# Shared query rows from a second DMA queue, folds on one engine, warming matmuls, and queries held behind keys in an attention and Fourier-mixing kernel

## The chip, the cores and the metric

The kernel runs on one core of a Trainium2 chip. A core has five engines with a queue of instructions each, worked off in order: TensorE (PE in the profile: matmuls, with the weight loads shown apart as PEld), VectorE (DVE), ScalarE (ACT), GpSimd (POOL) and SyncE (SP), which here only issues DMAs. The metric is the device time of one execution in microseconds; the median of the runs shown counts. A profiled execution has its own time, and its span runs from the first to the last instruction.

## The reference

All data are float32. Batch and heads are 8, the sequence 576, the head dimension 64.

```
q_s = exp(q - max over head dim);   q_s /= sum over head dim + 1e-9
k_s = exp(k - max over sequence);   k_s /= sum over sequence + 1e-9
x   = q_s @ (k_s.T @ v)             per head, then heads side by side: (8, 576, 512)
u   = x + real(fft over sequence (fft over the 512 columns (x)))
un  = (u - mean) / sqrt(variance + 1e-6)       per row
out = u + relu(un @ w_ch1) @ w_ch2             w_ch1: 512 x 2048, w_ch2: 2048 x 512
```

## The kernel before

**Tiling.** A batch has 576 rows. 512 of them form four tiles of 128 rows that are mirror images of one another for the Fourier transform; `xpart(b, c, u)` is tile (c, u) of batch b. The remaining 64 rows of each batch are "shared": those of all batches are gathered into one further group of rows, two batches (128 rows) at a time. Queries of a pair of batches for these rows are loaded by `t_rows` with the pieces that `shared` lists: one piece of four rows (0, 32, 64, 96 of the tile, at a stride in memory) and eight of 15 or 16 rows.

**Attention of one batch** (`attention`) is a software pipeline over items: four key items ("k", two heads each), four own query tiles ("q"), and for even batches one shared query tile ("t"). Stages of a key item: load, `k_exp` (maximum on VectorE, exponential with its sum on ScalarE), `k_turn` (five transposes on PE, a copy of four of them to `ks` by ScalarE, L451, and of the fifth by VectorE, L455), `k_times_v` (five matmuls, L463, then two scalings into `kvr`, L466). Stages of a query item: load, `q_exp` (maximum on VectorE L496, subtraction on GpSimd L497, exponential on ScalarE L498, sum, reciprocal and scaling on VectorE L500 to L503), `q_turn` (four transposes L509, a copy L516), `q_times_kv` (L541, a copy of x L543). The shared tile has `t_turn` and `t_fold` (into T and F), and `t_times_kv` closes the batch (L551, L557 and the value `g`, L559 to L562).

**Fourier mixing** (`transform`, `second`, `mix_own`, `mix_shared`). A transform over the sequence and one over the columns are made of folds (sums and differences of mirrored halves) and small matmuls with cosine and sine tables. `transform` first folds the four tiles into `eo[0]` to `eo[3]`: `tokens_folded` (L579), `columns_folded` (L584), `by_frequency` (L590), `columns_again` (L602, L603). The sums of the first two run on GpSimd, the differences on VectorE; `eo[2]` and `eo[3]` feed the sine blocks, `eo[0]` and `eo[1]` the cosine blocks. Then come five blocks of matmuls (L622, L625) in the order 2, 3, 0, 1, 4, each evicted by three ScalarE copies (L628 to L633). `second` multiplies by the column tables (L645, L648), and `added` adds the result to x (L663, L664).

**The feed-forward part.** Seven groups of 512 rows take it in Strassen form, with seven products instead of eight (`up` L814, `down` L850), reading prepared weights from memory. The first batch takes it plainly (`plain`): 16 up steps (L744, relu L746) and 64 down steps (L753). While it runs, the weights, which lie in memory as 64-bit words, are converted to float32 (`convert`: ScalarE L313 and L321, VectorE L314, L316, L318, GpSimd L322, 32 pieces), combined for Strassen (`combine`, L328 to L338) and written back to memory. Between the down steps lie the attention, mixing and norm of the second batch, placed by the list `gaps` (how many down steps before each further side step).

**Order.** The program writes steps in a fixed order; the framework then lists each engine's instructions by data dependences and expected costs, and inserts semaphore waits. `wait_for(t, raws)` adds an artificial dependence: VectorE operations that read a word of `t` and write back unchanged words of the named tiles, so that whatever uses these comes after `t`. Before the change it holds the first four weight pieces behind the folds (L596). `hold` keeps buffers of the second batch's keys and queries unused until the up steps 12 and 14. `first` issues all loads of the first batch on SP: keys 0 and 1, all values, keys 2 and 3, own queries, shared queries, tables, weights.

The second batch's third and fourth key, and its last query tile, use the space of the normalised input of the up stage (`spare`), which is free after its last matmul.

## Time and profile before

| | |
|---|---|
| median of 3 runs | 1154.71 us (1154.26 to 1156.3) |
| the profiled execution | 1154.03 us |
| its span | 1152.2 us |
| TensorE busy | 1099.4 us (95%) |
| VectorE busy | 556.5 us (48%) |
| ScalarE busy | 352.5 us (31%) |
| GpSimd busy | 378.3 us (33%) |
| first up matmul (L744) | at 63.41 us |
| first down matmul (L753) | at 121.35 us |
| first Strassen matmul (L814) | at 210.32 us |

The page gives busy times by engine, and the span in 40 slices with a digit for the busy share of each. "PEclk" is the TensorE clock that was granted, in tenths of full speed. In the timeline each row has a start and a length in us, then the engine, the line of the program, the operation, output and inputs by the program's names with their shapes, a count, and in brackets the idle time of the engine before it with what ended that. A row may merge several instructions. A float32 matmul appears as two records, so that a down step of one matmul with 512 columns is two records, 0.857 us together at full clock.

### The profile page before, as it was taken

What the parts mean: (1) busy time and instruction counts of PE and PEld (TensorE: products, weight loads), DVE (VectorE), ACT (ScalarE), POOL (GpSimd) and SP (SyncE); (2) the same over time, 40 slices, a digit from 0 to 9 for tenths busy, and PEclk for the clock granted to TensorE, in tenths of its full rate; (3) what the DMA queues carried; (4) which work ended last, traced back from release to release, by engine and by line L of the source; (5) the groups of instructions that cost most, each with busy time, mean ns of one, the idle gap of its engine ahead of it and who ended that gap; (6) DMA issues with size and microseconds to landing.
All of it is one profiled execution on the core that took longest, in us unless ns stands there. A gap on an engine that the chain in (4) does not pass through costs nothing.

```text
span 1152.2 us, 14397 instructions
## 1 busy us (share of the span) xinstructions
PE 1099.4 (95%) x5432; PEld 918.5 (80%) x5432; DVE 556.5 (48%) x1136; ACT 352.5 (31%) x699; POOL 378.3 (33%) x344
## 2 busy tenths in 40 slices
PE   6499799998999999999999999999999999999997
PEld 5444465787888988888889888888889888888886
DVE  6888748368343634376334733583434353202301
ACT  4575322344123512242225222341233142201200
POOL 3446624237103520255023601361033303402320
PEclk9789899999999999999999999999999999999999
DMA  8556777255345534553365434543454344444451
GB/s 293 168 168 212 247 275 229 80 187 187 140 142 201 202 113 145 185 188 146 120 206 196 154 116 153 200 178 137 142 181 151 115 140 171 165 155 153 148 183 55
DMA packets 92101, 193.75 MB, mean 168 GB/s; under 512 B 23296, under 2 KB 58624, under 8 KB 84864
## 3 DMA queue, kind: packets, MB, share of 16 engines
q1 hardware_dynamic: 90424, 192.05, 49.0%
q8 instruction: 43, 0.70, 0.2%
q10 hardware_dynamic: 1608, 0.79, 0.2%
q14 instruction: 26, 0.21, 0.1%
HBM read 168.69 MB, written 28.31 MB: 171 GB/s over the span
## 4 chain that ended last, share of the span: by engine, by line
PE 76%; DVE 8%; ACT 2%; POOL 1%; issue 1%; DMA 1%; DVEq 0%; POOLq 0%; SPq 0%
PE bb L814 13%; PE bb L850 13%; PE bc L850 10%; PE bc L814 8%; PE ba L814 8%; PE ba L850 7%; PE acc L463 2%; PE bc L753 2%; PE acc L541 2%; PE acc L622 2%; PE acc L625 1%; PE acc L645 1%; PE tr L714 1%; PE tr L450 1%; PE tr L509 1%; PE bb L753 1%
## 5 line engine op out<-in xcount | busy, mean ns | idle before, releaser
L814 PE MATMUL bb<-unT,big 128*128 128x256 f32 x768 | 187.8, 381 | 0.0
L850 PE MATMUL bb<-big 128*128 128x256 f32 x768 | 172.8, 379 | 0.0
L814 PEld LDWEIGHTS bb<-unT,big 128*128 128x128 f32 x768 | 142.8, 190 | 23.4 <-DVE u L782 4.0
L850 PEld LDWEIGHTS bb<-big 128*128 128x128 f32 x768 | 145.1, 190 | 20.0
L814 PE MATMUL bc<-unT,big 128*128 128x256 f32 x512 | 125.4, 379 | 0.0
L814 PE MATMUL ba<-unT,big 128*128 128x256 f32 x512 | 124.0, 379 | 0.0
L328 POOL TENSOR_TENSOR big<-big 128x512 f32<-128x512 f32 (+1 forms) x38 | 46.1, 1214 | 234.0 <-ACT big L826 233.6
L850 PE MATMUL bc<-big 128*128 128x256 f32 x512 | 116.5, 379 | 0.5 <-DVE x L867 0.5
L826 ACT ACTIVATE big<-big 128x512 f32<-128x512 f32 x96 | 60.5, 630 | 183.9 <-DVE big L825 183.4
L850 PE MATMUL ba<-big 128*128 128x256 f32 x512 | 114.1, 379 | 0.0
L850 PEld LDWEIGHTS bc<-big 128*128 128x128 f32 x512 | 95.9, 190 | 14.2 <-DVE x L867 0.9
L850 PEld LDWEIGHTS ba<-big 128*128 128x128 f32 x512 | 95.9, 190 | 12.3
L814 PEld LDWEIGHTS bc<-unT,big 128*128 128x128 f32 x512 | 95.4, 190 | 12.4
L814 PEld LDWEIGHTS ba<-unT,big 128*128 128x128 f32 x512 | 95.2, 190 | 11.8
L786 DVE TENSOR_TENSOR u<-bb,s 128x512 f32<-128x512 f32 x40 | 27.6, 690 | 141.1 <-PE bb L850 80.0
L336 POOL TENSOR_TENSOR unT<-unT 128x512 f32<-128x512 f32 x8 | 14.2, 1776 | 171.8 <-DVE unT L335 171.8
L862 POOL TENSOR_TENSOR x<-x,u 128x512 f32<-128x512 f32 x14 | 17.8, 1269 | 149.9 <-DVE u L786 118.8
L782 DVE TENSOR_TENSOR u<-bb,s 128x512 f32<-128x512 f32 x40 | 27.6, 691 | 79.7 <-PE bb L814 42.4
L825 DVE TENSOR_TENSOR big<-bc,u 128x512 f32<-128x512 f32 x64 | 44.1, 689 | 22.9 <-PE bc L814 22.0
L778 ACT COPY s<-ba 128x512 f32<-128x512 f32 x40 | 23.4, 586 | 90.3 <-PE ba L850 47.1
L497 POOL TENSOR_TENSOR q<-q,qm 128x512 f32<-128x512 f32 x30 | 31.5, 1058 | 58.7 <-DVE qm L496 30.3
L329 POOL TENSOR_TENSOR big<-big 128x512 f32<-128x512 f32 (+1 forms) x38 | 48.0, 1264 | 2.3 <-DVE big L330 0.4
(222 smaller groups left out, 1673.2 us busy)
## 6 DMA issues: line engine op xcount, KB each, us to landing
big<-w1s SPq DMA_DIRECT2D x64, 896.0 KB, 4.7
big<-w2s SPq DMA_DIRECT2D x56, 1024.0 KB, 4.9
big<-in_w_dram SPq DMA_DIRECT2D x21, 512.0 KB, 4.8
k<-in_kT_dram SPq DMA_DIRECT2D x26, 288.0 KB, 4.1
q<-in_q_dram SPq DMA_DIRECT2D x27, 256.0 KB, 2.8
v<-in_v_dram SPq DMA_DIRECT2D x26, 256.0 KB, 3.8
words<-in_w_dram SPq DMA_DIRECT2D x11, 512.0 KB, 10.4
w2s<-big SPq DMA_DIRECT2D x8, 512.0 KB, 10.4
```

What stands on the lines that cost most here:

```text
L328: e1.tensor_tensor(out=to(4), in0=at(2), in1=at(3), op=ALU.add)
L329: e1.tensor_tensor(out=to(2), in0=at(0), in1=at(2), op=ALU.subtract)
L463: nc.tensor.matmul(pk, lhsT=ks[:, c, :], rhs=v[:, c, :], start=(c == 0), stop=(c == NC - 1))
L497: nc.gpsimd.tensor_tensor(out=heads, in0=heads, in1=spread(m), op=ALU.subtract)
L753: nc.tensor.matmul(po[:], lhsT=h[:, f, i * P:(i + 1) * P], rhs=self.w2sb[:, f, :], start=(f == 0), stop=(f == NF - 1))
L778: nc.scalar.copy(temp("s1"), box["ba"][:])
L782: V.tensor_tensor(out=temp("u2"), in0=box["bb"][:], in1=box["s1"][:], op=ALU.add)
L786: V.tensor_tensor(out=temp("u3"), in0=box["bb"][:], in1=box["s1"][:], op=ALU.add)
L814: nc.tensor.matmul(bank()[:, i, :], lhsT=w[:, WA_AT[m], k * P:(k + 1) * P], rhs=unT[:, B_AT[m], k, :], start=first and i == 0 and k == 0, ...
L825: V.tensor_tensor(out=hp(i), in0=bank[:], in1=u[:], op=ALU.add)
L826: nc.scalar.activation(hp(i), hp(i), ACT.Relu)
L850: nc.tensor.matmul(bank()[:, i, :], lhsT=h[p][:, A_AT[m], i * P:(i + 1) * P], rhs=w[:, p, :], start=first and i == 0 and p == 0, stop=p == ...
```

## The change

All parts concern the first two batches, except that shared queries are loaded in fewer pieces everywhere.

- `t_rows`: four runs of 32 rows on an engine given by the caller, then the one piece of four rows on SP, which overwrites the first row of each run and so waits for it. In `first` the runs are issued by ScalarE ahead of everything, followed by a dummy exponential; the last piece goes out after the first half of the values. The values come in two halves by columns.
- The shared query item stands after the first two keys in the first batch, no longer at the end, and `t_times_kv` comes earlier (step 8).
- `transform` for the first batch: all folds on VectorE, first those of the sine parts (2, 3), then the cosine parts; the hold on the first four weight pieces moves behind the last fold. After each column fold two warming matmuls are issued (`warm`: the tile times the identity, into a PSUM buffer that nobody reads), and after each sum in `mix_own` three. They are ordinary matmuls of 256 columns.
- The second batch: when its third key is turned, `wait_for` makes its four query tiles depend on that key's copy. The copy of the fifth transpose of its keys is made by ScalarE.
- `gaps` begins 2, 2, 2, 2, 2, 8, 2, ... in place of 8, 2, 2, ...

As listed by engine in the built programs: TensorE's queue gets 20 warming matmuls; the second batch's first key transposes stand after 5 down matmuls (11 before); ScalarE's queue has the copies of keys 0 and 1 and the third key's exponential ahead of all query exponentials of that batch (before: three query exponentials ahead of the first copy); of the first four weight conversions VectorE's queue has one complete and the first step of another before the additions to x (before: all four).

```diff
+    def warm(self, t, n):
+        junk = self.turned()
+        for _ in range(n):
+            self.nc.tensor.matmul(junk[:, 0:2, :], lhsT=self.ident[:], rhs=t, start=True, stop=True)
...
+        last = self.t_rows(b, tail, nc.scalar)
+        t = self.small.tile([P, 1], F32, tag="root", name="root", bufs=1)
+        nc.scalar.activation(t[:], self.eps[:], ACT.Exp)
         for r in range(NR):
             load(ks[r], self.kT[b, r * P:(r + 1) * P, :])
-            if r == 1:
-                load(v[:, 0:4, :], self.v[b, 0:512, :].rearrange("(c p) n -> p c n", p=P))
-                load(v[:, 4, :], self.v[b, S - P:, :])
+            if r % 2 == 0:
+                cols = slice(r * P, (r + 2) * P)
+                load(v[:, 0:4, cols], self.v[b, 0:512, cols].rearrange("(c p) n -> p c n", p=P))
+                load(v[:, 4, cols], self.v[b, S - P:, cols])
+                if r == 0:
+                    last()
...
-    def t_rows(self, b, q):
-        for rows, mem in self.shared(self.q, b):
-            self.nc.sync.dma_start(q[rows], mem)
+    def t_rows(self, b, q, e):
+        flat = self.q.rearrange("b s n -> (b s) n")[b * S:(b + 2) * S]
+        for i in range(4):
+            at = i * S // 2 + P
+            e.dma_start(q[i * Q:(i + 1) * Q], flat[at:at + Q])
+        return lambda: self.nc.sync.dma_start(q[0:P:Q], flat[::S // 2])
...
-        items += tail + own if b else own + tail
+        items = items + tail + own if b else items[:2] + tail + items[2:] + own
...
-        return pipelined(items, stages) + [lambda: self.t_times_kv(b)]
+        steps = pipelined(items, stages)
+        steps.insert(len(steps) if b else 8, lambda: self.t_times_kv(b))
+        return steps
...
         nc.scalar.copy(ks[:, 0:4, :], pt[:])
+        if it[1:] == (1, 2):
+            self.wait_for(ks[:, 0, :], [q.bitcast(I32) for q in self.held_back])
...
-        nc.vector.tensor_copy(ks[64:, 4, :], pt[64:, 0, :])
+        copy = nc.scalar.copy if it[1] == 1 else nc.vector.tensor_copy
+        copy(ks[64:, 4, :], pt[64:, 0, :])
...
-            for i, (e, op) in enumerate(((G, ALU.add), (G, ALU.add), (V, ALU.subtract), (V, ALU.subtract))):
+            for i in some:
+                e, op = ((V if b == 0 else G), ALU.add) if i < 2 else (V, ALU.subtract)
                 t = eo[i]
                 e.tensor_tensor(out=t[:, 1:HD], in0=t[:, 1:HD], in1=t[:, D - 1:HD:-1], op=op)
+                if b == 0:
+                    self.warm(t[:, 0:HD], 2)
...
+        def at_first():
+            for some in ((2, 3), (0, 1)):
+                for f in (tokens_folded, columns_folded, by_frequency, columns_again):
+                    f(some)
+            t = self.small.tile([P, 1], F32, tag="root", name="root", bufs=1)
+            V.tensor_scalar(out=t[:], in0=eo[1][:, NN:NN + 1], scalar1=0.0, scalar2=None, op0=ALU.mult)
+            nc.scalar.activation(t[:], t[:], ACT.Sqrt)
+            self.wait_for(eo[1][:, NN:], [self.raws[i] for i in range(4)])
...
         def add(lo, hi):
-            self.added(self.xpart(b, c, 0), lo, hi)
-            self.added(self.xpart(b, c, 1), hi, lo)
+            for u, (f, g) in enumerate(((lo, hi), (hi, lo))):
+                x = self.xpart(b, c, u)
+                self.added(x, f, g)
+                if b == 0:
+                    self.warm(x[:, 0:HD], 3)
...
-            gaps = [8] + [2] * (len(one) - 1) + [3] * 5 + [1] * 4 + [2] * (len(two) - 9) + [1] * 7
+            gaps = [2] + [2] * 4 + [8] + [2] * (len(one) - 6) + [3] * 5 + [1] * 4 + [2] * (len(two) - 9) + [1] * 7
```

The same choice of engine and of `some` stands in `tokens_folded`, `by_frequency` and `columns_again`. The line numbers of the changed program are about 40 higher: L744 becomes L784, L753 L793, L463 L488, L656 L693, L814 L854, L509 L536.

## The prediction

> **What bounds the kernel now.** I read the page's 40 slices first, then the busy time by stretch, the list of waits, and the timeline around the two places where TensorE (PE) is idle. PE is busy 1099.4 of 1152.2 us, so at most 52.8 us of idling can be won, plus what runs at half clock. The slices put nearly all of it at the start and in the fourth and fifth slice:
>
> ```profile
> PE   6499799998999999999999999999999999999997
> DVE  6888748368343634376334733583434353202301
> PEclk9789899999999999999999999999999999999999
> ```
>
> By stretches of 4 us (columns: length, busy us and instructions of PE, weight loads, VectorE, ScalarE, GpSimd, then clock, DMA share, GB/s):
>
> ```profile
> core 0: us, PE busy (x) PEld busy (x) DVE busy (x) ACT busy (x) POOL busy (x), PEclk, DMA share, GB/s
> ...
> 12.00:16.00 4.00, 3.25 (x16) 2.88 (x16) 3.13 (x8) 2.61 (x5) 2.88 (x3) 1.00 0.37 81
> ...
> 36.00:40.00 4.00, 0.00 (x0) 0.00 (x0) 4.00 (x12) 0.00 (x1) 2.47 (x3) 0.59 0.27 69
> ...
> 52.00:56.00 4.00, 0.00 (x0) 0.00 (x0) 4.00 (x13) 1.63 (x3) 0.00 (x0) 0.72 0.57 209
> 56.00:60.00 4.00, 1.42 (x7) 1.42 (x8) 3.96 (x15) 0.86 (x3) 0.00 (x0) 0.50 0.00 0
> 60.00:64.00 4.00, 3.20 (x12) 2.08 (x11) 2.91 (x12) 3.82 (x8) 0.72 (x1) 0.50 0.00 0
> ```
>
> VectorE (DVE) is full while PE has nothing, and the clock is at half when the first dense matmuls (L744) begin at 63.41. The timeline of PE shows the price of that clock, eight matmuls in 5.67 us where the next eight take 3.60:
>
> ```profile
> 63.41 5.67 PE L744 MATMUL ba<-unT,big 128*128 128x512 f32 x8 [0.77 <-ACT unT L718]
> 68.92 3.60 PE L744 MATMUL bb<-unT,big 128*128 128x512 f32 x8
> ```
>
> The second place is the second batch's keys. First the timeline of PE, then that of ScalarE (ACT), in one stretch:
>
> ```profile
> 132.27 1.02 PE L753 MATMUL bc<-big 128*128 128x512 f32 x2
> 137.21 2.08 PE L463 MATMUL acc<-v,ks 128*128 128x128 f32 x8 [3.91 <-ACT ks L451]
> 140.44 0.80 PE L463 MATMUL acc<-v,ks 128*128 128x128 f32 x2 [1.16 <-DVE ks L455]
> ```
>
> ```profile
> 132.75 0.63 ACT L498 ACTIVATE q<-q 128x512 f32<-128x512 f32 x1 [1.99 <-POOL q L497]
> ...
> 136.05 0.63 ACT L498 ACTIVATE q<-q 128x512 f32<-128x512 f32 x1 [1.91 <-POOL q L497]
> 136.58 0.57 ACT L451 COPY ks<-tr 128x512 f32<-128x512 f32 x1
> ```
>
> The copy of the turned keys (L451) stands in ScalarE's queue behind query exponentials that wait for GpSimd; PE waits 3.91 us for it, and 1.16 more for the second copy on VectorE. To price this: the down stage runs from 121.35 to the first L814 at 210.32, 88.97 us. Its PE work at the undisturbed rates of the same timeline is 128 matmul records x 0.429 = 54.9 (3.43 us per eight), keys 4 x (0.55 + 1.11) = 6.6, queries 4 x (0.44 + 0.89) = 5.3, the shared part 1.8, five transform blocks 4.9, three mixes 3.4, turns 1.8: 78.7. So 10.3 us are lost, all between 131 and 151: 5.7 idle (3.91 + 1.16 + 0.67) and 4.6 of half clock.
>
> **What the Trainium skill says.** "TensorE: Matmul & The Clock Gate", section "What's actually happening": the array runs at half clock by default and at full clock after about 3.4 us of sustained activity; the trace agrees (0.50 between 56 and 64, full speed some 5 us into L744). "GPSIMD Engine Reference", section "1. Specifications": GpSimd shares its SBUF interface with VectorE instructions of two SBUF inputs; here L579 takes VectorE 1.21 us beside GpSimd against 0.69 for L503, of the same shape, alone. "DMA: Bandwidth & Descriptors", "Issuing engines are not separate DMA queues": a second issuing engine saves issue time only.
>
> **The front, part by part.** (a) Shared queries: nine pieces held the SP queue 9.07 us (5.07 to 14.14) and DMA sank to 81 GB/s between 12 and 16. Four runs now leave from ScalarE, one from SP. Own queries were fetched before that gap, so they gain nothing from it; tables and weights come up to 9 us earlier, but nobody waits for them. 0.26 MB more stand ahead of keys and own queries: with 336 to 388 GB/s, about +0.7 us. The exponential's table load (1.28, formerly after the first keys) moves ahead of them: about -0.5, hidden later. Taken together nothing, 0 to +1.
> (b) Until the last query is scaled VectorE has its old key and query work and now also the shared part: after the shared rows land (about 9.2, from the bytes ahead of them) two key maxima 1.5, copies 1.2, kv scaling 2.3, query maxima 3.4, sums 3.3, scaling 3.4, small ones 1.8, T and F 1.7, L586 to L589 1.0: 19.6 us. Before, it idled about 3 us in the same stretch; I allow 1, so 29.8 at worst, 29 taken. Then turn 0.63, copy 0.59, product 1.1 and five ScalarE copies of 0.52, partly behind each other: last x at about 34, against 32.0 before.
> (c) Folds on VectorE alone, without a neighbour: 4 x 0.65 + 4 x 0.36 + 4 x 0.37 + 8 x 0.24 = 7.4 us; those of tokens 0 start before the last x, 6 remain: done at 40 to 40.5, before at 41.5. GpSimd's six fold operations go, at no gain beyond this. Eight warming matmuls lie between (0.43 us each at full, 0.86 at half clock); they read what the next fold overwrites, so the last fold may wait 0.5.
> (d) Sines first: blocks 2 and 3 compute from about 38, but ScalarE holds the sqrt table load (1.28) and a value that needs the last fold; from 40.5 it still owes 1.9 (load and value) + five block evictions of 0.75 + three conversion passes of 0.63 = 7.5. First L693 at about 48.4, before (as L656) at 50.86: -2.5. The warm clock hides behind ScalarE here.
> (e) Adds 4.27 and norm 5.04 as before; two conversion steps (1.3) now lie between: VectorE done at 59.0 (before 60.17). Turns at full clock and two copies less ahead: 1.9 for 3.24. L784 (the old L744) starts at about 60.9: -2.5.
> (f) Twelve warming matmuls in the adds: if the clock is full at L784, 5.67 - 3.60 = 2.1 more. Sum of the front: -4.6; bounds +1 (VectorE idles as before, clock cold) and -8.
> (g) The first four conversions move: of their 12 VectorE steps about half come after the norm, some 4 us in a stage (63.4 to 121.35) where VectorE was busy 48.83 of 57.95. Hidden, if the idle 9 us can be filled.
>
> **The second batch.** Key steps come earlier (after 5 instead of 11 down steps), and the queries are held: a VectorE operation that reads the third key's copy writes into all four query tiles, so no query exponential can stand ahead of a key copy; the second copy goes to ScalarE, 0.3 behind the first. Now, from the end of the up stage t: PE reaches the first product (L488) at 5 x 0.857 + 0.55 + 2 x 0.857 = t + 6.5. ScalarE's queue puts the third key's exponential ahead of that copy, and this key's load waits for the up stage to free its buffer and for three query loads: issued at t + 1.5 to 3.3 (before: at t + 3.8), 4.1 to land, maximum 0.74, exponential 0.78, copies 0.9: t + 8 to 10. PE waits 1.5 to 3.5, say 3. Then nothing is late: third copy at t + 15.3, queries released, first one ready 5.5 later (maximum 0.7, GpSimd 1.3, exponential 0.63, sum to scaling 2.2) at t + 21, wanted at t + 26. VectorE is idle some 2 us behind the hold; the last conversion and the kv scaling stand behind it, wanted by nobody before t + 26. With 0.5 of other waits and a third of the half-clock loss (1.4), 4.9 of the 10.3 stay: -5.4. Bounds: -9 (no wait) and 0 (a cold clock and a late key). Further on, folds of this batch start when x is there and take 10.6 as before; PE has 16 us of other work in that place, so nothing becomes late. Later batches: four or five issues less on SP per shared load, where PE is 95 to 100% busy: nothing.
>
> **Sum.** 1154.0 (the profiled execution; span 1152.2) - 4.6 - 5.4 = 1144.0. The median shown is 0.7 above the profiled one: 1144.7. A measurement of this kernel can tell about 0.2%, 2.3 us.
>
> **Rivals.** (1) The stall only moves: the third key's load is what the copies wait for, the clock falls, and the second batch gains nothing; the front alone remains, 1154.7 - 4.6 = 1150. For it: copies still stand behind an exponential that needs a late load. Against: 4.1 us to land from an earlier issue. (2) The front is bound by VectorE all the way and is no shorter (bound +1); the second batch gives 5.4: about 1149. For it: VectorE is at 3.5 to 4.0 of 4 us in most stretches up to 60, and only GpSimd's folds are moved on to it. (3) Slower, by one mechanism: VectorE's conversions fall behind in the up stage, because its idle time there is made of waits in an in-order queue and can't be filled; each us that it is behind at t goes on the third key's maximum, its exponential, all key copies and PE. Beyond t + 6 each us is lost; with the half clock (4.6) and a front gain of 4.6 to eat, it decides from a lag of some 10 us on, and 13 us would give 1158. Against: only 4 us are moved there.
>
> **Chances and range.** Both gains, 1138 to 1149: 0.64. Rival 1: 0.14. Rival 2: 0.10. Rival 3: 0.12. Faster 0.80, same 0.08 (edges of rivals 1 and 2), slower 0.12. The range, 1138 to 1153, reaches from a front of -8 with a mid gain of -8.5 to the weak end of rivals 1 and 2. The likeliest case alone: 1138 to 1149.
>
> **What would show it.** Right: L784 starting near 61 with eight records in 3.6 us; VectorE without GpSimd beside it in the folds, 0.65 each; first L693 near 48; PE's wait before L488 below 4 us and no query exponential ahead of a key copy; clock 1.00 through the down stage; down stage about 84 us. Wrong: a start later than 63, a clock of 0.5 at L784, waits of more than 6 us at L488 or any at L536, VectorE conversions still running 10 us after the up stage, or new PE waits at the transform blocks or the first L854.

## The result, and the profile after

The changed kernel takes 1156.57 us (median, 1154.65 to 1157.65), the kernel before 1155.51 us in the same comparison (1154.26 to 1156.31): a ratio of 1.0008, 95% interval 0.9991 to 1.0026. Nothing was won that can be measured; the prediction was 1144.7 us. The profiled execution took 1157.65 us, its span is 1155.9 us.

The slices of the changed kernel, PE, VectorE and granted clock, answer to the first lines of the prediction:

```profile
PE   5789889999999999999999999999999999999997
DVE  6788856469243634466334832483434343202201
PEclk9999989999999999999999999999999999999999
```

A slice is 28.9 us here. The second rises from 4 to 7, the fifth, where the keys stalled, from 7 to 8 (the prediction named the fourth and the fifth; the fourth stood at 9 in both kernels). But the first falls from 6 to 5, and the third and the sixth from 9 to 8: idle time has moved there. The clock is up in nearly all. By stretches of 4 us in the front (same columns as in the prediction):

```profile
12.00:16.00 4.00, 3.54 (x16) 3.14 (x16) 3.13 (x10) 1.98 (x4) 0.66 (x1) 1.00 1.03 385
36.00:40.00 4.00, 2.67 (x9) 1.66 (x8) 3.16 (x8) 0.59 (x1) 0.00 (x0) 0.86 0.01 3
52.00:56.00 4.00, 4.00 (x21) 3.51 (x20) 4.00 (x13) 0.84 (x3) 0.00 (x0) 1.00 0.26 107
56.00:60.00 4.00, 2.23 (x15) 1.45 (x13) 4.00 (x13) 1.59 (x4) 0.95 (x1) 1.00 0.00 0
60.00:64.00 4.00, 0.78 (x6) 0.42 (x4) 4.00 (x13) 3.05 (x6) 0.52 (x1) 1.00 0.42 131
64.00:68.00 4.00, 3.57 (x5) 1.60 (x6) 4.00 (x8) 4.00 (x8) 2.55 (x2) 0.57 0.30 74
```

DMA moves 385 GB/s where it sank to 81, and PE is busy with warming matmuls and transposes up to 61.6 us. Then it idles until 64.4, and the clock is 0.57 just when the dense matmuls begin. PE's timeline and its list of waits from 50 to 230 us (columns: who waited for whom, us in total, times, longest) say why, and what else is new:

```profile
64.43 5.36 PE L784 MATMUL ba<-unT,big 128*128 128x512 f32 x8 [2.85 <-DVE big L335]
69.62 2.74 PE L784 MATMUL bb<-unT,big 128*128 128x512 f32 x6
```

```profile
PE bc L793 <- POOL big L339: 3.2, 1, 3.2
PE ba L784 <- DVE big L335: 2.9, 1, 2.9
PE acc L568 <- ACT qT L543: 2.8, 1, 2.8
...
PE acc L488 <- ACT ks L472: 1.2, 1, 1.2
```

The wait for the key copy has shrunk from 3.91 + 1.16 to 1.2 us. Three others stand beside it: those before the first up product (L784) and the first down product (L793) were 0.77 us each in the kernel before, and that before the first query product of the second batch (L568) is new. None of the three was in the prediction.

*The first up product.* Its transposed inputs are complete at 62.6, it starts at 64.43. What it waits for, L335, is the last VectorE step of the third weight piece. Up step 0 writes PSUM bank `ba`, and `convert` puts the third piece into the same bank (`ba` is one of the buffers in PSUM, the memory that matmuls write). In the kernel before this conversion was over long before the up stage (VectorE ran it from 44.7 to 47.8 us); now it comes after the norm.

*The first down product.* In the kernel before it waited, too, but little:

```profile
121.35 1.96 PE L753 MATMUL bc<-big 128*128 128x512 f32 x4 [0.77 <-issue]
```

ScalarE's timeline says for what, first before, then after:

```profile
120.10 0.63 ACT L313 ACTIVATE acc<-words 128x512 f32<-128x512 f32 x1 [1.83 <-DMA words<-in_w_dram]
120.67 0.58 ACT L746 ACTIVATE big<-bc 128x512 f32<-128x512 f32 x1
121.26 1.28 ACT L440 ACT_TABLE_LOAD   x1
```

```profile
120.52 0.63 ACT L330 ACTIVATE acc<-big 128x512 f32<-128x512 f32 x1 [3.38 <-DMA big<-in_w_dram]
121.09 0.65 ACT L338 ACTIVATE big<-big 128x512 int32<-128x512 uint32 x1
121.75 1.28 ACT L461 ACT_TABLE_LOAD   x1
123.05 0.78 ACT L461 ACTIVATE k<-k,km 128x576 f32<-128x576 f32 x1
...
123.82 0.57 ACT L786 ACTIVATE big<-bc 128x512 f32<-128x512 f32 x1
```

The first down product writes bank `bc`, which the relu of the 15th up step frees. In both kernels this relu stands in ScalarE's queue behind the conversion of a weight that DMA has not brought yet: before the change the relu is done at 121.25, and the first down product starts at 121.35. In the changed kernel the framework lists the table load for the keys' exponentials and the first of these ahead of the relu as well: it runs at 123.82 for 0.57 us, and the first down product starts at 124.50. The list of waits names GpSimd (L339), whose step ended at 123.96; ScalarE's relu ends later, at 124.39, and with another bank for this product the wait is gone (below). "Perfetto Trace Analysis", section "Tensor Engine Instruction (MATMUL, LD_WEIGHTS)", of the Trainium skill says that ScalarE, VectorE and GpSimd work off their queues strictly in order. The trace agrees: ScalarE idles 3.38 us for a DMA while this relu, which doesn't need it, stands behind.

*The first query product.* ScalarE's timeline shows what stands ahead of the first query copy (L543), and PE's what that costs:

```profile
148.62 0.63 ACT L525 ACTIVATE q<-q 128x512 f32<-128x512 f32 x1 [0.97 <-POOL q L524]
151.00 0.63 ACT L525 ACTIVATE q<-q 128x512 f32<-128x512 f32 x1 [1.74 <-POOL q L524]
155.88 0.63 ACT L525 ACTIVATE spare<-spare 128x512 f32<-128x512 f32 x1 [4.25 <-POOL spare L524]
156.53 0.59 ACT L543 COPY qT<-tr 128x512 f32<-128x512 f32 x1
```

```profile
157.17 2.26 PE L568 MATMUL acc<-kvr,qT 128*128 128x128 f32 x8 [2.76 <-ACT qT L543]
159.22 1.06 PE L536 MATMUL tr<-ident,q 128*128 128x128 f32 x4
160.07 3.54 PE L793 MATMUL ba<-big 128*128 128x512 f32 x4
```

The hold keeps query exponentials from standing ahead of the copies of the first three keys. It lets the last query's exponential (on `spare`) stand ahead of the first query's copy: the same stall one stage further on, with the same half clock behind it (eight L568 records in 2.26 us, at full clock 1.05; four L793 in 3.54, at full clock 1.88).

Summed by stage starts, the first profile of each kernel and, below, a second one (columns in us; "to the end" is from the first Strassen matmul to the end of the span):

| | first up | first down | first Strassen | to the end | span |
|---|---|---|---|---|---|
| before | 63.41 | 121.35 | 210.32 | 941.9 | 1152.2 |
| before, again | 64.36 | 121.64 | 210.56 | 941.3 | 1151.9 |
| changed | 64.43 | 124.50 | 213.98 | 941.9 | 1155.9 |
| changed, again | 63.63 | 122.85 | 210.71 | 942.7 | 1153.4 |

Executions of one kernel differ by some us (those of the kernel before lay between 1151.5 and 1159.6 us over all comparisons), so a difference of 1 or 2 us between two single profiles says little; the verdicts below rest on the ratios, the profiles show the places.

### The profile page after: what moved, and what is told of

Same layout as the page of the kernel before. It is cut to its first block, busy times and chain, and to the rows that moved or that the text cites. A ratio compares the mean times of both kernels' runs of the same rounds, so it can differ in the third digit from the quotient of the medians.

```text
span 1155.9 us, 14469 instructions
## 1 busy us (share of the span) xinstructions
PE 1106.0 (96%) x5472; PEld 922.9 (80%) x5472; DVE 558.2 (48%) x1142; ACT 353.4 (31%) x704; POOL 373.4 (32%) x338
## 3 DMA queue, kind: packets, MB, share of 16 engines
q10 hardware_dynamic: 1800, 1.05, 0.3%
## 4 chain that ended last, share of the span: by engine, by line
PE 75%; DVE 8%; ACT 2%; POOL 2%; issue 2%; DMA 1%; POOLq 0%; ACTq 0%; SPq 0%
PE bb L854 13%; PE bb L890 13%; PE bc L890 10%; PE bc L854 8%; PE ba L854 8%; PE ba L890 7%; PE acc L568 2%; PE acc L488 2%; PE bc L793 2%; PE acc L659 2%; PE acc L662 1%; PE acc L682 1%; PE tr L754 1%; PE tr L536 1%; PE ba L793 1%
## 5 line engine op out<-in xcount | busy, mean ns | idle before, releaser
L854 PE MATMUL bb<-unT,big 128*128 128x256 f32 x768 | 187.8, 381 | 0.0
L854 PEld LDWEIGHTS bb<-unT,big 128*128 128x128 f32 x768 | 142.9, 190 | 23.4 <-DVE u L822 4.0
L854 PE MATMUL bc<-unT,big 128*128 128x256 f32 x512 | 125.1, 379 | 0.0
L854 PE MATMUL ba<-unT,big 128*128 128x256 f32 x512 | 124.3, 379 | 0.0
L854 PEld LDWEIGHTS bc<-unT,big 128*128 128x128 f32 x512 | 95.5, 190 | 12.5
L854 PEld LDWEIGHTS ba<-unT,big 128*128 128x128 f32 x512 | 95.0, 190 | 11.7
L524 POOL TENSOR_TENSOR q<-q,qm 128x512 f32<-128x512 f32 x30 | 32.6, 1090 | 53.5 <-DVE qm L523 25.6
```

The source lines that it names most:

```text
L524: nc.gpsimd.tensor_tensor(out=heads, in0=heads, in1=spread(m), op=ALU.subtract)
L854: nc.tensor.matmul(bank()[:, i, :], lhsT=w[:, WA_AT[m], k * P:(k + 1) * P], rhs=unT[:, B_AT[m], k, :], start=first and i == 0 and k == 0, ...
```

## The experiments

The theory at the outset: each cured wait hands the time to the next place in some engine's queue (a gate, below, is such a place, where one stage must wait for another), first the PSUM bank, then the relu, then the key copies, then the query copies. The first rival: one part of the change costs what the others win. The second: VectorE and GpSimd, full with conversions and combinations, set the pace whatever the order.

### The parts of the change alone

**The third weight piece in another bank:**

```diff
-            n = ("bb", "bc", "ba", "bb")[i] if i < 4 else "acc"
+            n = ("bb", "ba", "bc", "bb")[i] if i < 4 else "acc"
```

> The changed kernel with one line different: the second weight piece is converted in PSUM bank ba and the third in bc, instead of bc and ba. Theory (the first up matmul waits for the third conversion only because both use bank ba; and the relu of the 15th up step stands behind the first key exponential): the first up matmul starts about 1.8 us earlier, near 62.7; in the built order the relu now stands ahead of that exponential, so the first down matmul no longer waits 3.2 us; together 3 to 7 us less than the changed kernel, part of it taken back before the first key product L488. Rival (VectorE's conversions are the bound, wherever the waits show): the same end within 2 us, with the wait moved to L488.

Measured: 1155.62 us, ratio 1.0002 (0.9993 to 1.0012). The bank wait is gone (PE waits 1.15 us, for the transposed input). The first up product still comes at 63.78, not near 62.7: that is 0.65 us ahead of the first profile of the changed kernel and level with its second, so the 1.7 us of the bank are read from the waits, not from the starts. The first down product comes at 121.93. But PE then waits 4.2 us before the first key product (1.2 in the changed kernel) and 3.3 before the first query product: what is won there is not kept one stage later.

**The second batch's part on the kernel before:**

```diff
+        if it[1:] == (1, 2):
+            self.wait_for(ks[:, 0, :], [q.bitcast(I32) for q in self.held_back])
...
-        nc.vector.tensor_copy(ks[64:, 4, :], pt[64:, 0, :])
+        copy = nc.scalar.copy if it[1] == 1 else nc.vector.tensor_copy
+        copy(ks[64:, 4, :], pt[64:, 0, :])
...
-            gaps = [8] + [2] * (len(one) - 1) + ...
+            gaps = [2] + [2] * 4 + [8] + [2] * (len(one) - 6) + ...
```

> The kernel before with only the second batch's part of the change: queries held behind the third key, second key copy on ScalarE, the new gaps. Theory (the hold moves the stall from the keys to the queries, whose turned copies stand behind the last query exponential, and the relu of the 15th up step stands behind a key exponential): within 3 us of the kernel before; PE waits 3 us or more at the queries, and the down stage takes 85 to 90 us. Rival (the new front ruins the second batch, which by itself gains 5.4): about 1149.

Measured: 1158.83 us, ratio 1.0033 (1.0022 to 1.0044), slower. PE waits 3.8 us before the first key product and 4.3 before the first query product. The key wait that the hold was to remove is as long as before it; the query wait is new. (Its single profile starts the up stage at 66.03, 2.6 us later than the first one of the kernel before, in code that the edit leaves alone; the ratio rests on 14 executions.)

**The front's part alone**, which is the change without the hold, with the second key copy on VectorE and the old gaps:

```diff
-        if it[1:] == (1, 2):
-            self.wait_for(ks[:, 0, :], [q.bitcast(I32) for q in self.held_back])
...
-        copy = nc.scalar.copy if it[1] == 1 else nc.vector.tensor_copy
+        copy = nc.vector.tensor_copy
...
-            gaps = [2] + [2] * 4 + [8] + [2] * (len(one) - 6) + ...
+            gaps = [8] + [2] * (len(one) - 1) + ...
```

> The changed kernel without the second batch's part: no hold, second key copy on VectorE, the old gaps. Theory (the front itself gains nothing at the first up matmul because of the PSUM bank, and puts about two conversions more into the up stage): first up matmul at 64 to 65, up stage 59 to 61 us, end 1 to 6 us above the kernel before. Rival (the front gains as predicted and the second batch loses it): about 1150.

Measured: 1170.96 us, ratio 1.0134 (1.0116 to 1.0153). **And the change without the hold only** (the first two lines of that diff):

> The changed kernel without the hold of the queries behind the third key, everything else kept. Theory: a query exponential comes to stand ahead of key copies again; the wait before the first key product, 1.2 us in the changed kernel, becomes 4 to 6, the one before the first query product (2.8) goes below 1, and the half clock moves with it: 1156 to 1159, so the hold only chooses where the stall lies. Rival (the hold removes a stall): without it 4 to 6 us are lost more than the query side gains, 1160 or more.

Measured: 1170.26 us, ratio 1.0128 (1.0114 to 1.0142). Both lose some 14 us against the changed kernel, so with this front the hold saves that much; my expectation for the second (1156 to 1159) was far off, and its rival right in sign. Some 7 us are lost in the down stage (97.0 us in the second, 89.5 in the changed kernel): PE waits 4.0 us at the keys, and 4.9 at a transform block, whose copies stand behind an exponential of the third batch's keys. The other 6 lie after the first Strassen matmul (947.9 us to the end in place of 941.9), where the third batch follows, which neither edit touches. What differs there shows in the run with three holds below.

**The change without its 20 warming matmuls:**

```diff
-                if b == 0:
-                    self.warm(t[:, 0:HD], 2)
...
-                if b == 0:
-                    self.warm(x[:, 0:HD], 3)
```

> The changed kernel without its 20 warming matmuls. Theory (they shorten the transform blocks by about half, some 4 us of PE, most of it hidden behind ScalarE, but the clock is cold again at the first up matmul): first VectorE addition (L693) 1 to 3 us later, first up matmul 0.5 to 3 us later, clock at the first up matmul as low as with them; end 0 to 3 us above the changed kernel. Rival (they hold the folds on VectorE and cost more than they give): 0.5 to 1 us less.

Measured: 1158.68 us, ratio 1.0033 (1.0018 to 1.0049). The granted clock from 54 to 66 us is 0.50, with the warming 1.00 up to 60 and 0.87 after it. But at the place that the warming was for nothing is gained:

```profile
63.33 5.34 PE L780 MATMUL ba<-unT,big 128*128 128x512 f32 x8 [0.72 <-issue]
```

The first eight up matmuls take 5.34 us without it and 5.36 with it, and the first up product comes at 63.33, earlier than with it (64.43 and 63.63). Of the theory the low clock there and the end came true, the later starts did not. The bank wait is gone, too: VectorE begins the third weight piece at 48.65 here, ahead of the norm, so the edit has changed an order besides. What is longer is the down stage (90.7 us in place of 89.5 and 87.9), with a wait of 3.9 us before the first key product. The ratios differ by 0.25%, some 3 us, and their intervals overlap: that the warming is worth anything is not shown.

### Curing one gate after the other

**Both bank edits:** the third weight piece as above, and the first down product in the bank that the 14th relu frees.

```diff
-                t = ("ba", "bc", "bc", "bb")[i]
+                t = ("ba", "bb", "bb", "bc")[i]
```

> The changed kernel with two edits of PSUM banks: the third weight piece in bank bc (as in the run before with that bank), and the first down product in bank bb, which the 14th step of the up stage frees, in place of bc, which the 15th frees behind an activation that waits for a weight's DMA and, in the changed kernel, behind a table load and a key's exponential. Theory (waits lie one behind the other in ScalarE's order, so that the next one takes back what one cure gives): PE's wait before the first down product, 1.3 us with the first edit alone, goes to below 0.5, but the third key's exponential, which stands ahead of the first key copy, comes no earlier: the wait before L488 grows from 4.2 to about 5, and the time stays at 1155 to 1156. Rival (the first down product's bank is itself what costs): the stage from the first down product to the first Strassen product keeps its 90.4 us and starts 1.3 to 2 us earlier, time 1153.5.

Measured: 1155.76 us, ratio 0.9998 (0.9990 to 1.0006). The first up product starts at 61.53 with the clock up, and the first down product at 116.54, 4.8 us earlier than in the kernel before and without a wait:

```profile
116.54 3.60 PE L793 MATMUL bb<-big 128*128 128x512 f32 x8
119.97 1.02 PE L793 MATMUL bc<-big 128*128 128x512 f32 x2
...
129.77 2.50 PE L488 MATMUL acc<-v,ks 128*128 128x128 f32 x10 [6.12 <-ACT ks L472]
```

Then the first key product waits 6.12 us, and the first Strassen matmul comes at 209.90, about where it came before (210.32 and 210.56). The copy (L472) stands behind the third key's exponential, this behind its maximum, and VectorE's timeline shows what the maximum stands behind:

```profile
126.30 0.93 DVE L347 TENSOR_TENSOR big<-big 128x256 f32<-128x256 f32 x1 [1.16 <-POOL big L345]
127.26 0.43 DVE L348 TENSOR_TENSOR big<-big 128x256 f32<-128x256 f32 x1
127.60 0.75 DVE L459 TENSOR_REDUCE km<-spare 128x1 f32<-128x576 f32 x1
```

Strassen combinations of the weights, which GpSimd feeds: it is busy, with them and one conversion step, without a break from 118.0 to 126.9 us. In this trace the keys' time is set there and not by PE. The theory held in the main (a wait of about 5, time unchanged).

**As that, and three more holds:** the third and fourth key behind the first and second key's copy, the last query behind the first query's copy.

```diff
+        if it[1:] in ((1, 0), (1, 1)):
+            self.wait_for(ks[:, 0, :], [self.live["k", 1, it[2] + 2][0].bitcast(I32)])
...
+        if it[1:] == (1, 0, 0):
+            self.wait_for(qT[:, 0, :], [self.held_back[3].bitcast(I32)])
```

> As the run before it, and three holds more: the third and fourth keys may be touched by VectorE only when the first and second key's first copy is there, and the last query only when the first query's copy is there. That puts the key copies and the first query copy ahead of these exponentials in ScalarE's order, and changes nothing else. Theory (ScalarE's order, copies behind exponentials that wait for VectorE and GpSimd, is what PE waits for): the wait before L488 falls from 4.2 to 1.5 or less, that before the first query product from 3.3 to 1 or less, the half clock after each goes (some 3 us together), the later third key and last query give back 2 to 3: 1147 to 1150. Rival (VectorE and GpSimd, full with conversions and Strassen combinations, are late whatever the order): the waits come back before the third key's and the last query's turns, gain below 2 us: 1154.

Measured: 1158.30 us, ratio 1.0024 (1.0014 to 1.0034): a miss. The first key product waits only 0.4 us, but the second waits 3.1, again behind the third key's exponential, and the query product waits 2.0 for VectorE's scaling of the last key product and 1.1 for its copy. The down stage is 1.7 us shorter. But then the program takes 948.7 us from the first Strassen matmul on, 6.9 more. With the holds the framework lists the third batch's instructions in another order. GpSimd's timeline, and PE's behind it:

```profile
258.75 1.72 POOL L345 TENSOR_TENSOR big<-big 128x512 f32<-128x512 f32 x1
260.55 1.27 POOL L346 TENSOR_TENSOR big<-big 128x512 f32<-128x512 f32 x1
261.77 1.27 POOL L347 TENSOR_TENSOR big<-big 128x512 f32<-128x512 f32 x1
263.12 1.27 POOL L348 TENSOR_TENSOR big<-big 128x512 f32<-128x512 f32 x1
264.35 1.04 POOL L526 TENSOR_TENSOR q<-q,qm 128x512 f32<-128x512 f32 x1
```

```profile
268.09 1.09 PE L538 MATMUL tr<-ident,q 128*128 128x128 f32 x4 [3.73 <-DVE q L532]
```

Two query subtractions (L526) stand behind four combinations; in the changed kernel, where the line is L524, all five stand ahead of them:

```profile
263.38 1.37 POOL L524 TENSOR_TENSOR q<-q,qm 128x512 f32<-128x512 f32 x1 [2.31 <-DVE qm L523]
266.02 1.27 POOL L345 TENSOR_TENSOR big<-big 128x512 f32<-128x512 f32 x1 [1.26 <-ACT big L866]
```

The runs of the front alone and without the hold have exactly this order, the same wait of 3.7 us in the third batch, and 948.5 and 947.9 us to the end.

**As that, and the first two conversions earlier, the next two later:**

```diff
+        if it == ("q", 0, 1, 1):
+            self.wait_for(q, [self.raws[0], self.raws[1]])
...
-            self.wait_for(eo[1][:, NN:], [self.raws[i] for i in range(4)])
...
-                    self.wait_for(un, [self.raws[i] for i in range(4, 11)])
+                    self.wait_for(un, [self.raws[i] for i in range(2, 11)])
```

> As the run before it, and the first two weight conversions may start when the last query is scaled (VectorE idles 4.7 us between 31 and 37), the third and fourth only after the norm. Theory (VectorE sets the front from the mixes to the norm, with two conversion steps between them): the first up product starts 1 to 1.5 us earlier (63.8 with the bank edit alone, so 62.3 to 62.8), the time is 1 to 1.5 below the run before. Rival (these steps lie in VectorE's own idle time, and the folds that now start behind two conversions give it back): first up product at 63.8 or later, no gain.

Measured: 1154.71 us, ratio 0.9990 (0.9982 to 0.9998). Faster than the run before it, but not by the mechanism expected: the first up product comes at 61.63 (61.29 there), as the rival said, since the folds now end at 44.2 in place of 41.8. The program has 945.4 us from the first Strassen matmul to the end in place of 948.7, and that is most of the gain. GpSimd has the same order in the third batch here (two subtractions behind four combinations), and PE's longest wait there is 2.6 us, for another step of a query, so this order by itself doesn't fix the 6.9 us.

**Both bank edits with the gaps of the kernel before:**

```diff
-            gaps = [2] + [2] * 4 + [8] + [2] * (len(one) - 6) + ...
+            gaps = [8] + [2] * (len(one) - 1) + ...
```

> The changed kernel with the two bank edits (as in the run with the down product's bank) and with the gaps of the kernel before: the second batch's key steps start after eight down steps in place of two, the queries keep their place. Theory (the changed kernel calls the keys some 5 us before the third key's exponential, which stands ahead of their copies, can be there, because its maximum waits on VectorE behind combinations that GpSimd feeds): the wait before L488, 6.1 us with the new gaps, falls below 1, the half clock behind it goes, and the stage from the first down product to the first Strassen product takes 86 to 88 us in place of 93.4. In this build GpSimd's order in the third batch puts two query subtractions behind four combinations, as it was in the runs without the hold and with three holds more, where the rest of the program took 948 in place of 942: time 1153 to 1156. Rival (the stage is bound at its end, by the queries, wherever the keys stand): the stage keeps 92 to 93 us, the wait before the first query product grows by what the keys gain, and the time is 1159 or more.

Measured: 1156.58 us, ratio 1.0003 (0.9992 to 1.0014). The down stage shrinks to 87.4 us, as expected, and the rest is 947.1, near the 948 expected. But in this profile the first up product comes at 64.00 and its first eight matmuls take 5.68 us, though the front and its banks are those of the run with both edits (61.53, 3.67 us); the first down product comes at 121.02 in place of 116.54. The first key product waits no more; the third does (1.8 us), and the fourth:

```profile
146.38 0.63 ACT L525 ACTIVATE q<-q 128x512 f32<-128x512 f32 x1 [4.45 <-POOL q L524]
147.38 0.63 ACT L525 ACTIVATE q<-q 128x512 f32<-128x512 f32 x1 [0.37 <-POOL q L524]
148.38 0.63 ACT L525 ACTIVATE q<-q 128x512 f32<-128x512 f32 x1 [0.37 <-POOL q L524]
149.03 0.58 ACT L472 COPY ks<-tr 128x512 f32<-128x512 f32 x1
```

```profile
149.67 2.26 PE L488 MATMUL acc<-spare,ks 128*128 128x128 f32 x10 [4.32 <-ACT ks L472]
```

The hold is let go by the *third* key's copy, so three query exponentials stand ahead of the *fourth* key's: the stall that the hold was to cure, one key later.

**As that, with the moved conversions** (diff above), and then **with the third and fourth query held behind the first query's copy**:

```diff
+        if it[1:] == (1, 0, 0):
+            self.wait_for(qT[:, 0, :], [q.bitcast(I32) for q in self.held_back[2:]])
```

> As the run with the old gaps, and the first two weight conversions start when the last query is scaled, the next two after the norm. Theory: the down stage is again 86 to 88 us; the first up product starts within 0.5 us of 61.5; and in this build GpSimd's order in the third batch has only one combination ahead of the third query subtraction, so the rest is again near 942: 1147 to 1151. Rival (the order in the third batch isn't what makes the rest longer): rest 945 or more, 1154 and up.

> As the run before it, and the third and fourth query of the second batch are held until the first query's copy is there, so that their exponentials can't stand ahead of it. Theory: the wait before the first query product (2.9 us with both bank edits) falls below 1 with the half clock behind it; the held queries are late by 1 at most: 2 to 4 us below the run before it. Rival (VectorE's kv scaling and GpSimd's combinations are late at this place whatever the order): the wait comes back before the first query product from the kv scaling or before the third query's turn, no gain.

Measured: 1153.89 us, ratio 0.9983 (0.9975 to 0.9992), and 1155.00, ratio 0.9990 (0.9977 to 1.0003). In the first the rest is 943.8 us, with the third batch's order that has one combination ahead of the third query. But the first up product comes at 64.05 and not near 61.5, since the folds, behind two conversions on VectorE, end at 46.6 us (42.0 in the run with both bank edits). PE waits 3.7 us at the first key and 4.9 at the fourth, and the down stage is 90.0, not 86 to 88. Before the first query product PE waits in neither run; in the second 7.2 us of waits stay at the keys: no gain.

**The hold behind the fourth key:**

```diff
-        if it[1:] == (1, 2):
+        if it[1:] == (1, 3):
```

on the run with old gaps and moved conversions, and then with the last query held behind the first query's copy (as in the run with three holds):

> As the run with old gaps and moved conversions (1153.9 us), and the queries of the second batch are held behind the fourth key's first copy in place of the third's. Theory (the wait follows the place of the hold: three query exponentials, released by the third key's copy, stand ahead of the fourth key's copy): the wait of 4.9 us before the fourth key's product goes below 1, the queries start some 3 us earlier or later than there and are wanted at about 150 us; the down stage takes 85 to 88 us in place of 90, time 1149 to 1152. Rival (VectorE and GpSimd are late whatever the order): the queries are late by the same time, PE waits 4 us or more before the first query's turn or product, time 1153.5 or more.

> As the run before it, and the last query is held behind the first query's copy. Theory: the first query product waits 1 us less than in the run before it or not at all, the last query isn't late: equal to 1.5 us faster. Rival: the last query's turn becomes late, up to 2 us slower.

Measured: 1152.04 us, ratio 0.9981 (0.9970 to 0.9991), and 1151.26 us, ratio 0.9966 (0.9955 to 0.9977): slightly faster than the kernel before. The wait at the fourth key is gone in both, and the down stage takes 87.0 and 88.7 us. The intervals of the two overlap, so the hold of the last query is not shown to gain. PE's list of waits in the second:

```profile
PE acc L488 <- ACT ks L472: 3.7, 1, 3.7
PE tr L538 <- DVE qrec L528: 2.1, 1, 2.1
```

**The key order turned round as well** (the hold of the third and fourth key, from the run with three holds), on the best run:

> As the best run so far (hold behind the fourth key, last query behind the first), and the third and fourth key may be touched by VectorE only after the first and second key's first copy. Theory of order: the wait of 3.7 us before the first key product goes, the third key's product is not later than 144: 1148 to 1150. Rival (backlog): VectorE puts the third key's maximum behind the combinations that GpSimd feeds, the third key's copy comes later than 146, PE waits there as long: 1151 to 1154.

Measured: 1152.79 us, ratio 0.9971 (0.9961 to 0.9981). The first key product no longer waits, the second waits 6.0 us: VectorE, held, puts the third key's maximum behind still more combinations (137.18, in the best run 132.59). The time is the rival's, and the combinations do stand ahead; the third key's copy comes at 144.3, earlier than it said. Whether they must stand ahead of that maximum, or only do so in VectorE's list, no run shows.

**The second batch's order on the kernel before:**

```diff
+        if it[1:] == (1, 3):
+            self.wait_for(ks[:, 0, :], [q.bitcast(I32) for q in self.held_back])
...
-        nc.vector.tensor_copy(ks[64:, 4, :], pt[64:, 0, :])
+        copy = nc.scalar.copy if it[1] == 1 else nc.vector.tensor_copy
+        copy(ks[64:, 4, :], pt[64:, 0, :])
...
+        if it[1:] == (1, 0, 0):
+            self.wait_for(qT[:, 0, :], [self.held_back[3].bitcast(I32)])
...
-                t = ("ba", "bc", "bc", "bb")[i]
+                t = ("ba", "bb", "bb", "bc")[i]
```

> The kernel before with the second batch's part alone: its old gaps, the queries held behind the fourth key, the last query behind the first query's copy, the second key copy on ScalarE, the first down product in bank bb. Front and conversions are those before. Theory (the changed front, with its banks mended, is worth about 2 to 3 us, the order of the second batch the rest): 1153 to 1154, so 2 us faster than before and 2 to 3 slower than the best run. Rival (the front is worth nothing, all is the order): 1151.

Measured: 1152.21 us, ratio 0.9964 (0.9955 to 0.9974), level with the best run on the changed front, so not by the expected 2 to 3 us behind. The first down product comes at 119.45 without a wait, about 2 us earlier than before, and the down stage keeps its length (88.7 us; 89.0 and 88.9 before), so that the whole moves with it. In that stage the waits for the second copies (1.16 and 0.67 us) are gone, but the one at the first key is as long as ever (3.91), and one before a query's turn has come:

```profile
PE acc L468 <- ACT ks L452: 3.9, 1, 3.9
PE tr L516 <- DVE qrec L508: 2.5, 1, 2.5
```

So by the profiles the gain arises at the first down product, whose bank was changed. Whether the order of keys and queries is needed to keep it through the stage would show in a run of the kernel before with this bank edit alone; there is none. The ratio says 4 us; where the other 2 lie, single profiles do not show.

**Each kernel once more:**

> The kernel before, once more, for a second profile. If the stage starts belong to the kernel, the first up product is within 0.5 us of 63.41 and the first down product of 121.35. If they belong to the execution (TensorE's granted clock falls in one and not in the other), they differ by 1 to 3 us with the clock in the stretches before them, as in the two runs with this front: 66.0 and 123.0, 64.4 and 119.4.

> The changed kernel, once more, for a second profile. The wait of 2.9 us before the first up product (the third weight piece's PSUM bank) and that of 3.2 before the first down product are of order and stay; the first up product comes at 63.0 to 63.5 where the clock is not down between 33 and 36 us, in place of 64.43, and the first down product 1 to 2 us earlier than 124.50.

The second profile of the kernel before begins its up stage 1 us later, but with the clock up:

```profile
64.36 3.67 PE L744 MATMUL ba<-unT,big 128*128 128x512 f32 x8 [0.77 <-ACT unT L718]
```

So it should reach the first down product about 1 us earlier (2.00 saved on eight matmuls, 0.95 later at the start), and reaches it 0.3 us later (121.64). PE waits 2.11 us there, 0.77 in the first profile: in the kernel before, the first down product is set by the 15th relu (done at 121.54; 121.25 in the first profile) and by the weight in front of it. A change of 1 us in the stages ahead disappears in this wait. In the second profile of the changed kernel the waits of 2.9 and 2.4 us at the two banks and of 2.8 at the query copy are there again: they belong to the order, not to the execution.

The stage starts of all runs, in us, with the ratio to the kernel before:

| | first up | first down | first Strassen | to the end | ratio |
|---|---|---|---|---|---|
| bank of the third piece | 63.78 | 121.93 | 212.26 | 942.1 | 1.0002 |
| second batch alone | 66.03 | 122.96 | 213.66 | 943.3 | 1.0033 |
| front alone | 64.87 | 125.32 | 218.48 | 948.5 | 1.0134 |
| no warming | 63.33 | 122.54 | 213.26 | 942.5 | 1.0033 |
| both banks | 61.53 | 116.54 | 209.90 | 941.8 | 0.9998 |
| + three holds | 61.29 | 116.30 | 208.00 | 948.7 | 1.0024 |
| + conversions | 61.63 | 116.64 | 208.40 | 945.4 | 0.9990 |
| no hold | 63.02 | 124.03 | 220.99 | 947.9 | 1.0128 |
| both banks, old gaps | 64.00 | 121.02 | 208.37 | 947.1 | 1.0003 |
| + conversions | 64.05 | 119.05 | 209.06 | 943.8 | 0.9983 |
| + two queries held | 62.94 | 117.98 | 210.16 | 943.7 | 0.9990 |
| conversions, hold at key 4 | 63.68 | 118.69 | 205.65 | 944.3 | 0.9981 |
| + last query held | 62.70 | 117.71 | 206.44 | 944.2 | 0.9966 |
| + keys first | 63.25 | 118.26 | 207.38 | 944.1 | 0.9971 |
| before, ordered | 64.44 | 119.45 | 208.10 | 941.9 | 0.9964 |

## Why the prediction was wrong

The prediction summed two gains, 4.6 us in the front and 5.4 in the second batch, and had 0.64 on their coming together. Neither came: the first down product was to come 4.6 us earlier and comes 3.2 us later in the first pair of profiles and 1.2 in the second; the down stage was to be 5.4 us shorter and is 0.5 us longer in the first pair and 1.1 shorter in the second.

**(a) and (b), loads and attention: 2 to 3 us short, and (a) not in size only.** It was put at nothing. But SP's piece of four rows waits for the four runs to land, and all loads behind it in SP's queue wait with it:

```profile
SPq L287 <- DMA big<-in_q_dram: 2.9, 1, 2.9
```

The own queries are issued at 9.44 us, before the change at 3.75, and the second key's maximum starts at 8.01, where before both first maxima were done at 5.1. The last query is scaled at 31.0 us, where 29 was taken and 29.8 called the worst. How much of that is the SP wait, no run without it shows.

**(b) to (d), folds, blocks: right in mechanism, up to 3 us off in size.** The last x is there at 36.8 us (36.0 in the second profile; "about 34" was said), since PE waits 1.2 us for a PSUM buffer before the last two query products, and these run at a clock of 0.62 in the first profile; the folds end at 43.2 and 42.4 (40 to 40.5 said); the first L693 is at 49.53 and 48.74 (48.4 said; 50.86 before). The folds do run at 0.65 us without a neighbour. Two sums do not come out as written: (d) makes 48.0 and not 48.4 (40.5 + 7.5), and in the second batch the steps of the first query make 4.8 and not 5.5. Both are small beside what failed.

**(e) VectorE's norm ends at 60.8 and 60.0 us** (59.0 said): 11.3 us from L693 on, where 10.6 were summed. The start of L784 at 60.9 became 64.43 and 63.63. Of these 3.5 and 2.7 us, 1.7 are the bank of the third weight piece (2.85 us of wait against 1.15 with the bank edit); the rest is the lateness of (a) to (e).

**(f) Full clock at L784: it failed, and its cause is open.** The clock is up at the warming matmuls (1.00 from 54 to 60 us), but the first eight matmuls take 5.36 and 5.35 us where 3.60 was expected. The longer wait for the bank lies between, but it is not shown to be the cause: 5.37 and 5.68 us came with waits of only 1.15 and 0.77 (third piece's bank; both banks, old gaps), the other eight runs with bank edits on the changed front took 3.67, and so did the second profile of the kernel before, with no warming at all.

**(g) "Hidden" is the step that failed first.** The moved conversions do find time on VectorE, as was worked out. But they also hold PSUM banks and stand in queues, and these were not counted: the third piece is converted in the bank of up step 0. With both banks mended the first down product came at 116.54, where 121.35 - 4.6 = 116.75 was predicted. Some of that agreement is luck: the first up product was 0.6 us later than said, and a wait of 0.77 us before the first down product, which the prediction had not counted, was gone. The same front with the old gaps gave 121.02.

**The unspoken step behind the whole front sum failed as well: that what the front wins, the end wins.** The kernel before already had a gate at the first down product, the 15th relu behind a weight's DMA at 120.10; PE waited only 0.77 us there, and the row was read past. In the two profiles of the kernel before and in that with the second batch's order, the conversion ahead of this relu starts at 120.10, 120.41 and 120.89 us, while PE is ready at 120.58, 119.53 and, going on by another bank, 119.45: 1 us of PE doesn't move it. How much of 4.6 us would have been lost there no run shows; with the changed front and both bank edits this relu was done at 118.93, 2.4 us after PE was ready. The change made that gate later: a table load and an exponential came ahead of the relu (2.1 us, from 121.74, when the weight's second step is done, to 123.82). The earlier key steps are not the whole reason: the front's part alone, with the old gaps, has this order too, and the run with the third piece's bank, with the new gaps, has not. And with the gate cured there was the next, the wait before the first key product.

**The second batch: "Then nothing is late" failed.** With t taken as the start of the first down product, the wait before L488 (1.5 to 3.5 said; 1.2 and 1.9 measured) and the third copy at t + 15.3 (15.5 measured) were about right. But the first query was ready at t + 27.5, not t + 21: its maximum came 3.4 us after the copy that releases it, behind conversions and combinations on VectorE, and the scaling of the query took its turn among them. And its copy stood behind the last query's exponential. The prediction looked for exponentials ahead of *key* copies only; it did not write out ScalarE's order for the *query* copies, where three rows stand ahead of the first. The stage took 89.5 and 87.9 us; 83.6 was predicted, and the shortest of any run was 87.0.

**The rivals.** The first (the stall only moves) and the second (the front is no shorter) are both what happened, though by other mechanisms than those named, and each was counted alone: 1150 and 1149. Together they give 1154.7, or 1155.7 with the second one's bound of +1. Of the third (conversions fall behind) the sign came and the consequence did not: GpSimd's step of the last conversion ends at 144.9 us, in the kernel before at 129.1, but the third key's maximum starts at 132.00 where it was 131.74. Of the signs named as "wrong", L784 after 63 us and half clock there did show it, as did the new wait at L536 (1.2 us).

**What is settled and what is open.** Shown by runs: the two bank dependences; that the stall follows the holds (to the first query, to the fourth key); that without the hold this front loses some 14 us, 6 of them after the first Strassen matmul. Argued from traces, and not shown by a run that changes it alone: that GpSimd's combinations set the third key's maximum, and that GpSimd's order in the third batch makes the up to 7 us there. Open: what the warming is worth, what keeps the clock down at L784, and what the changed front is worth with all gates mended. The best run on it and the kernel before with the second batch's order are level (0.9966 and 0.9964), but the first has 2.3 us more after the first Strassen matmul. On the changed front the first up product came at 61.29 to 61.63 in the three runs with both bank edits and the new gaps, but at 62.70 to 64.05 in the six with the old gaps; with the front before it came at 63.41 to 66.03 in four profiles. Why the gaps, which come later, go with that, is open, too.

## What to carry to other kernels

Before a gain is added up, find the next place where the stages meet, a PSUM bank or a copy in another engine's queue, and read the time of its releaser: a wait of 0.8 us there may be a gate that swallows a part of what is won earlier. A hold that keeps one kind of instruction from standing ahead of another must last until the last of those it protects: here the third of four keys let it go. When a framework orders the instructions, compare its order in the stages that the edit doesn't touch as well: here edits in the second batch came with 6 to 7 us more after it.

## What the runs showed of the hardware

The granted clock differs between executions of one program at the same place. From 33 to 36 us, the first and the second profile of the changed kernel:

```profile
33.00:36.00 3.00, 2.99 (x17) 2.99 (x18) 1.12 (x2) 1.51 (x3) 0.00 (x0) 0.62 0.89 227
```

```profile
33.00:36.00 3.00, 2.47 (x18) 2.28 (x19) 1.12 (x2) 2.41 (x5) 0.00 (x0) 1.00 1.06 284
```

The clock is 0.62 in one and 1.00 in the other, and sixteen small matmul records (L568) take 3.18 us in the first and 2.05 in the second. The last x comes 0.8 us later in the first (36.82 against 36.01). The first eight dense matmuls of the kernel before take 5.67 us in one execution and 3.67 in another. The Trainium skill ("TensorE: Matmul & The Clock Gate", section "What's actually happening") says that the activity window runs freely and that the count of slow matmuls depends on its phase. A count that differs between executions agrees with that; the window itself no trace here shows. The lower clock cost 1.1 us at these small matmuls and 2.0 at the dense ones.
